# A ranking step of an attention kernel moved from VectorE to GpSimd, and its score matmuls cut in two equal halves

## The chip, the cores and the metric

The kernel runs on one core of a Trainium2 chip. The metric is the device time of one launch in microseconds (us). The engines are TensorE (PE, with its weight loads shown apart as PEld), VectorE (DVE), ScalarE (ACT), GpSimd (POOL) and SyncE (SP). Each works through its own instructions in the order in which the program gives them; semaphores tie the engines together.

## The reference

Attention with a top-32 mask comes first, then two mixture-of-experts (MoE) layers on its output:

```python
# q, k, v: batch 2, heads 8, 576 rows, 64 columns
scores = scale * np.matmul(q, k.transpose(0, 1, 3, 2))
kth = np.partition(scores, -32, axis=-1)[..., -32:-31]
scores = np.where(scores >= kth, scores, -1e9)
attn = np.exp(scores - scores.max(-1, keepdims=True))
attn = attn / (attn.sum(-1, keepdims=True) + 1e-9)
out = np.matmul(attn, v)
# then x = out as (1152, 512); per layer: 8 experts, each token goes to its best expert,
# relu(x @ w1[e]) @ w2[e], times the gate's probability; the first layer has a capacity
```

The change lies in the attention part alone: for each row of scores the 32nd largest value is wanted as a threshold.

## The kernel before

Attention works in blocks of 128 rows of scores by 576 keys. Two heads form a unit; a unit has 9 blocks (4 full row tiles of each head, and one block that holds the 64 last rows of both heads and so needs twice the score matmuls). There are 8 units, 72 blocks, numbered by their place in `seq`, and 36 pairs of blocks, numbered k_.

For each block PE multiplies queries and keys into PSUM (`scores`). The keys are held in two parts, a rounded one and its remainder, so a block has two passes. The result goes to two places: keys 512 to 575 beside the transposes in `pt_`, keys 0 to 511 in a bank of `sc`. ACT copies both to SBUF (`s`). DVE reduces a pair's 576 scores to 160 candidates in a row (`folds`: two maxima, two minima, one more maximum, then four searches for the eight largest). Then DVE ranks them (`chain`): four times it takes the eight largest of the candidates into `top`, and between these it replaces the eight that were found by -1e30 (a match-replace, which the trace shows as a load of the values and the replacement). The eighth value of the fourth step is the threshold. The two chains of a pair are interleaved with the folds of the next pair (`woven`).

From the largest value and the threshold POOL forms `nb` (`limits`) and a shifted copy of the scores (`lowered`); ACT forms a mask (`below`). PE transposes the shifted copy and adds the mask in PSUM (`flip`), ACT takes the exponential (`expo`), PE multiplies by the values (`values`), ACT copies the result out.

The program orders this by hand. In iteration i of the main loop PE issues the scores of block i + 4, then the flip of block i - 3, then the values of block i - 4, and then jobs: turning the next unit's queries and keys (`turn`, six times in a unit; `turn_tails`, whose last transpose is L288; `v_turn`; `v_gates`). DVE issues in two iterations the folds of the next pair and the chains of the present one. POOL's queue holds in each iteration the limits, the shifted copy and jobs: the splits of queries and keys, sums, `normed` (whose output SP sends to memory) and `missed`, which notes in `flv` whether a block's candidates could have lost a value. The last four blocks are written out behind the loop: the last two chains run on DVE alone, their rows are kept as they are and transposed by PE. At the end PE sums `flv`; where a block is flagged, a loop (`repair`) does it again. The MoE layers start when attention has ended.

Of the kernel before, what the change touches and what calls it, by code (L numbers as in the profile page):

```python
# [10 lines left out]
F32 = mybir.dt.float32  # L11
F32R = mybir.dt.float32r
BF = mybir.dt.bfloat16
# [3 lines left out]
OP = mybir.AluOpType  # L17
# [5 lines left out]
TOPK = 32  # L23
NEG = -1.0e30
BIG = 2.0 ** 80
EPS = 1e-9
SIZES = [256, 208, 192, 176, 160, 144, 128, 128]
COLS = [(r, t, min(128, n - t * 128)) for r, n in enumerate(SIZES) for t in range((n + 127) // 128)]
# [19 lines left out]
def attn_moe_moe_kernel(ctx, tc, q, k, v, g1, w11, w12, capacity, g2, w21, w22, out):  # L48
# [113 lines left out]
    def attention():  # L162
# [9 lines left out]
        with tc.tile_pool(name="ald", bufs=2) as ld, tc.tile_pool(name="awk", bufs=2) as wk, \  # L172
# [21 lines left out]
            for i in range(4):  # L194
# [2 lines left out]
                nc.gpsimd.memset(v_[:, :, :, D + E:], 1.0)  # L197
                vx.append(v_)
            flv = wk.tile([128, NU, NT, 2], F32, name="flv", bufs=1)
            xb = ps.tile([128, 512], F32, name="xb")  # L200
            pt_ = ps.tile([128, NC * 128], F32, name="pt")
            rest_read = []
            xo = xb[:, :6 * XW].rearrange("p (g h w) -> p g h w", h=2, w=XW)
            zero = wk.tile([128, RW], F32, name="zero", bufs=1)
# [100 lines left out]
            def scores(u, t):  # L305
                z = st[u]
                if tiles[t] is not None:
                    hh, c = tiles[t]
                    ops = [(z["qk"][:, hh, 0, c * 128:(c + 1) * 128], z["qk"][:, hh, j]) for j in (1, 2)]
                else:  # L310
                    qt = z["qtail"].rearrange("p h s -> p (h s)")
                    ops = [(qt[:, hh * 128:hh * 128 + 128], z["qk"][:, hh, j]) for hh in range(2) for j in (1, 2)]
                k_, j_ = divmod(seq.index((u, t)), 2)
                z_ = pair(k_)
                sc, s = z_.sc, z_.s
                places_ = ((pt_[:, M * 128:S], slice(M * 128, S)), (sc[:, j_], slice(0, M * 128)))
                for n_, (l, r) in enumerate(ops):
                    for w_, (o, w) in enumerate(places_):
                        m_ = nc.tensor.matmul(o, l, r[:, w], start=(n_ == 0), stop=(n_ == len(ops) - 1))  # L319
                        if w_ and j_ and z_.read is not None:  # L320
                            tc.declare_no_dep(m_.ins, z_.read.ins, reason="two banks")
                for w_, (o, w) in enumerate(places_):
                    a_ = nc.scalar.activation(s[:, j_, w], o, AF.Copy)
                    if w_ == 0:
                        rest_read[:] = [a_]
                z_.read = a_
# [28 lines left out]
                            lambda j=j: nc.vector.max(x[:, j, W4 + 8:], z.mn[:, j])]  # L355
                return ops

            def chain(i):
                z = pairs[i // 2]
                x, t8 = z.cand[:, i % 2], z.top[:, i % 2]  # L360
                y = wk.tile([128, CW], F32, name="y")
                ops = []
                for r in range(TOPK // 8):
                    cur = x if r == 0 else y
                    w = t8[:, 8 * r:8 * r + 8]
                    ops.append(lambda w=w, cur=cur: nc.vector.max(w, cur))  # L366
                    if r < TOPK // 8 - 1:
                        ops.append(lambda w=w, cur=cur: nc.vector.match_replace(y, w, cur, NEG))
                return ops

            def woven(chains, fill, order=""):

# [275 lines left out]
            def run_jobs(i, late):  # L648
                for f, a in jobs.get(i, []):
                    if (f in turning or f == wide) == late:  # L650
                        f(*a)
                        flush()
# [2 lines left out]
                run_jobs(i, True)  # L655
            K = L // 2

            def back(k, wait=lambda: None):

                pt = flip(k)  # L660
                wait()
                if k >= 1:
                    value(k - 1)
                pTs[k] = expo(pt)
                if k >= 1:
                    value_out(k - 1)

            def fresh(k):
                lowered(*ranges(k))
                return lambda: below(*ranges(k))  # L670
# [14 lines left out]
            def keep(k, e):  # L685
                z = pairs[k // 2]
                nc.vector.scalar_tensor_tensor(kept[k % 2][:, :S], z.s[:, k % 2], z.top[:, k % 2, TOPK - 1:], e,
                                               op0=OP.is_ge, op1=OP.mult)

            for i in range(L - 4):  # L690
                k_, j_ = divmod(i, 2)
                if j_ == 0 and k_ >= 1:
                    limits(k_ - 1)
                relu = fresh(i - 2) if i >= 2 else lambda: None
                run_jobs(i, False)
                scores(*seq[i + 4])
                if k_ == 0:
                    vec = woven((chain(i), []), folds(j_, (1,) if j_ == 0 else (0, 1)))
                elif j_ == 0:
                    todo = woven((chain(i), chain(i + 1)), folds(k_ + 1, (0, 1)))  # L700
                    vec, todo = todo[:12], todo[12:]
                else:
                    vec = todo
                do(vec)
                if i >= 3:
                    back(i - 3, relu)
                else:
                    relu()
                run_jobs(i, True)
                if i < 4:  # L710
                    wide_spin((6, 6, 6, 3)[i], xb)
                elif i == 4:
                    spin(12, free)
# [20 lines left out]
            value_out(L - 5)  # L734
            pTs[L - 4] = expo(flip(L - 4))
            run_jobs(L - 3, True)
            limits(K - 2, slice(1, 2))
            relu = fresh(L - 3)
            a, b = chain(L - 2), chain(L - 1)
# [1067 lines left out]
```

## Time and profile before

| what | us |
|---|---|
| median of 3 runs (lowest, highest) | 613.36 (613.05, 617.69) |
| the profiled execution, its own time | 613.21 |
| its span, first to last instruction | 611.6 |
| DVE busy | 501.1 (82%) |
| PE busy | 587.1 (96%) |
| ACT busy | 417.5 (68%) |
| POOL busy | 191.9 (31%) |

The span is what the profile shows; about 1.6 us lie around it. The busy shares are means over the whole span, and the attention stage fills only its first 268 us or so. The ends of matmuls are modelled, so PE's work is better read from the distance between the starts of its instructions. "Idle before" is time in which the engine did nothing ahead of an instruction, with the instruction that ended it. The granted clock of TensorE was 0.986 of its full 2.4 GHz as a mean over the span.

### The profile page before, as it was taken

The page shows a single profiled execution, that of the slowest core. Times are in us where ns is not written, and L with a number is a line of the kernel's source. Part 1 is how long each engine was busy: PE and PEld are TensorE (multiplying, and loading weights), DVE is VectorE, ACT ScalarE, POOL GpSimd, SP SyncE. Part 2 cuts the span into 40 slices and gives each one's busy share as a digit, 9 for nine tenths or more (in the row PEclk, how much of TensorE's full clock was granted, in tenths as well). Part 3 has the DMA queues.
Part 4 walks back from the last instruction along what each step waited for, and adds up shares of the span by engine and source line. Part 5 has one row for each costly group of instructions (what it writes and reads, how often), then busy time and mean ns, then how long its engine had stood idle before and what let it go on. Part 6 is the DMA issues. An engine that isn't in the chain of part 4 may idle for free.

```text
span 611.6 us, 13886 instructions
## 1 busy us (share of the span) xinstructions
PE 587.1 (96%) x4789; PEld 545.5 (89%) x4789; DVE 501.1 (82%) x1729; ACT 417.5 (68%) x970; POOL 191.9 (31%) x423
## 2 busy tenths in 40 slices
PE   8999999999999998879899999999999999999995
PEld 5789999999999988767799999999999899999994
DVE  6989999999999999974967778873478788788750
ACT  6668888888888876622776777764265678787650
POOL 8565554745374233424020200100012302111010
PEclk9989999999999999989899999999999999999999
DMA  6630332234350000019795568768276975777660
GB/s 144 158 70 10 109 95 81 70 91 71 103 51 18 4 18 4 10 38 303 268 342 211 187 232 241 238 232 294 107 240 217 343 258 189 264 267 253 220 217 14
DMA packets 78639, 96.04 MB, mean 157 GB/s; under 512 B 33797, under 2 KB 40453, under 8 KB 78560
## 3 DMA queue, kind: packets, MB, share of 16 engines
q1 hardware_dynamic: 73632, 84.07, 44.0%
q0 software_dynamic: 3728, 10.70, 5.4%
q8 instruction: 40, 0.66, 0.4%
q10 hardware_dynamic: 1200, 0.30, 0.2%
q14 instruction: 39, 0.32, 0.2%
HBM read 82.32 MB, written 13.22 MB: 156 GB/s over the span
## 4 chain that ended last, share of the span: by engine, by line
PE 37%; DMA 10%; issue 5%; DVE 1%; POOLq 0%; ACT 0%; POOL 0%; SPq 0%; ACTq 0%; DVEq 0%
PE pp L1095 8%; DMA out_dram<-yr,sidx 8%; PE pp L1134 7%; PE pp L1097 3%; PE pp L1136 3%; PE pp L1088 2%; DMA raw<-in_moe_w_dram 2%; PE pl L1148 1%; PE pt L1052 1%; PE pp L1128 1%; PE pp L1132 1%; PE pp L1130 1%; PE pp L1131 1%; PE pp L1091 1%; PE pp L1093 1%
## 5 line engine op out<-in xcount | busy, mean ns | idle before, releaser
L423 PE MATMUL xb<-vx,pT 128*128 128x73 f32 (+1 forms) x800 | 94.6, 267 | 0.4 <-ACT xl L436 0.4
L1095 PE MATMUL pp<-xT,w1c 128*128 128x416 f32 (+4 forms) x320 | 93.9, 362 | 0.5 <-DVE xT L1058 0.5
L423 PEld LDWEIGHTS xb<-vx,pT 128*128 128x128 f32 (+1 forms) x800 | 87.7, 182 | 2.7 <-issue 1.1
L1134 PE MATMUL pp<-hT,w2c 128*128 128x416 f32 (+4 forms) x320 | 88.0, 353 | 0.0
L1023 DVE TENSOR_TENSOR w2c<-raw,w2c 128x512 fp32r<-128x512 f32 x112 | 74.1, 685 | 16.8 <-ACT w2c L1022 16.6
L1136 PE MATMUL pp<-hT,w2c 128*128 128x208 f32 (+4 forms) x320 | 78.4, 245 | 0.0
L1097 PE MATMUL pp<-xT,w1c 128*128 128x208 f32 (+4 forms) x320 | 77.8, 243 | 0.0
L1023 DVE TENSOR_TENSOR w1c<-raw,w1c 128x512 fp32r<-128x512 f32 x96 | 60.9, 686 | 14.2 <-ACT w1c L1022 13.9
L1022 ACT ACTIVATE w2c<-raw 128x512 fp32r<-128x512 f32 x112 | 66.7, 623 | 6.7 <-PE pp L1136 3.7
L402 PE MATMUL pt<-ident,shifted 128*128 128x128 f32 x350 | 67.8, 279 | 0.6 <-ACT pT L411 0.3
L1074 ACT ACTIVATE t<-pp 128x208 f32<-128x208 f32 (+4 forms) x120 | 37.6, 314 | 41.3 <-PE pp L1097 29.6
L403 PE MATMUL pt<-negid,under 128*128 128x128 bf16 x350 | 63.8, 220 | 0.3 <-ACT under L393 0.3
L1022 ACT ACTIVATE w1c<-raw 128x512 fp32r<-128x512 f32 x96 | 53.5, 621 | 13.2 <-DMA raw<-in_moe_w_dram 7.1
L1095 PEld LDWEIGHTS pp<-xT,w1c 128*128 128x128 f32 x320 | 60.1, 188 | 1.5 <-DVE xT L1058 0.9
L1136 PEld LDWEIGHTS pp<-hT,w2c 128*128 128x128 f32 x320 | 61.2, 191 | 0.0
L1097 PEld LDWEIGHTS pp<-xT,w1c 128*128 128x128 f32 x320 | 61.1, 191 | 0.0
L1134 PEld LDWEIGHTS pp<-hT,w2c 128*128 128x128 f32 x320 | 60.2, 188 | 0.0
L366 DVE MAX8 top<-y 128x8 f32<-128x160 f32 x216 | 59.1, 313 | 0.0
L393 ACT ACTIVATE under<-s,nb 128x576 bf16<-128x576 f32 x70 | 53.7, 768 | 6.4 <-POOL nb L385 6.4
L402 PEld LDWEIGHTS pt<-ident,shifted 128*128 128x128 f32 x350 | 49.3, 141 | 5.2 <-POOL nb L680 0.8
L396 POOL TENSOR_SCALAR shifted<-s,nb 128x576 f32<-128x576 f32 x70 | 52.0, 746 | 4.1 <-POOL nb L385 0.2
L319 PE MATMUL sc<-qkT 128*128 128x512 f32 x128 | 53.0, 480 | 0.0
(332 smaller groups left out, 1447.5 us busy)
## 6 DMA issues: line engine op xcount, KB each, us to landing
raw<-in_moe_w_dram SPq DMA_DIRECT2D x62, 1024.0 KB, 5.5
out_dram<-zero SPq DMA_DIRECT2D x3, 768.0 KB, 3.8
y<-yr POOLq DMA_DIRECT2D x8, 256.5 KB, 4.2
kraw<-in_k_dram SPq DMA_DIRECT2D x8, 256.0 KB, 3.4
vraw<-in_v_dram SPq DMA_DIRECT2D x16, 128.0 KB, 2.9
vx<-in_v_dram SPq DMA_DIRECT2D x16, 128.0 KB, 2.6
w2c<-in_moe_w_dram SPq DMA_DIRECT2D x4, 512.0 KB, 8.0
x<-xn SPq DMA_DIRECT2D x15, 128.0 KB, 1.8
```

The costliest lines, as they stand in the source:

```text
L319: m_ = nc.tensor.matmul(o, l, r[:, w], start=(n_ == 0), stop=(n_ == len(ops) - 1))
L366: ops.append(lambda w=w, cur=cur: nc.vector.max(w, cur))
L393: nc.scalar.activation(under[k % 3][:, :S], s, AF.Relu, bias=nb[:, 1:2], scale=-BIG)
L402: both = (nc.tensor.matmul(pt[:, o], shifted[k % 3][:, o], ident, is_transpose=True, start=True, stop=False), nc.tensor.matmul(pt[:, o], u ...
L403: nc.tensor.matmul(pt[:, o], under[k % 3][:, o], negid, start=False, stop=True))
L423: nc.tensor.matmul(o, pT[:, c2, cols], z["v"][:, c2, hh], start=(c2 == 0), stop=(c2 == NC - 1))
L1022: nc.scalar.activation(o[:, 0], src_, AF.Copy)
L1023: nc.vector.tensor_tensor(o[:, 1], src_, o[:, 0].bitcast(F32), op=OP.subtract)
L1095: nc.tensor.matmul(ph[:, :2 * n].rearrange("p (w n) -> p w n", w=2), w[f][:, 0, d], xT[:, d, :, :n], start=st, stop=False)
L1097: nc.tensor.matmul(ph[:, :n], w[f][:, 1, d], xT[:, d, 0, :n], start=False, stop=sp)
L1134: nc.tensor.matmul(py[:, :2 * n].rearrange("p (w n) -> p w n", w=2), w[f][:, 0, o], hT[:, f, :, :n], start=st, stop=False)
L1136: nc.tensor.matmul(py[:, :n], w[f][:, 1, o], hT[:, f, 0, :n], start=False, stop=sp)
```

## The change

For pairs 2 to 33 the first removal of each chain leaves DVE. The first eight maxima (`heads`) are taken at the end of the DVE work of the pair before. POOL compares the candidates with the eighth value, writes 2^100 where a candidate is at least as large and 0 elsewhere (`gone`, bf16), and subtracts that from the candidates (`removed`). The chains go on from the second maximum (`tails_of`), behind the folds instead of interleaved with them. A tie at the eighth place would remove more than eight, so PE counts the removed in each pair by four matmuls with one column (`counted_out`), between the flip and the values. `ties` adds the counts up and raises the flags of a pair with too many; it stands behind the flip of block 68, ahead of the last two chains.

The score matmuls write keys 288 to 575 and then keys 0 to 287, both passes of a half one after the other. The right half has a place of its own behind the transposes' PSUM tile.

```diff
+OUT = 2.0 ** 100
...
+            unit = wk.tile([128, 1], BF, name="unit", bufs=1)
+            nc.gpsimd.memset(unit, 1.0 / OUT)
+            ones_f = wk.tile([128, 128], F32, name="ones_f", bufs=1)
+            nc.gpsimd.memset(ones_f, 1.0)
...
-            pt_ = ps.tile([128, NC * 128], F32, name="pt")
+            both_ = ps.tile([128, NC * 128 + W2], F32, name="pt")
+            pt_, right_ = both_[:, :NC * 128], both_[:, NC * 128:]
...
-                places_ = ((pt_[:, M * 128:S], slice(M * 128, S)), (sc[:, j_], slice(0, M * 128)))
-                for n_, (l, r) in enumerate(ops):
-                    for w_, (o, w) in enumerate(places_):
+                places_ = ((right_, slice(W2, S)), (sc[:, j_, :W2], slice(0, W2)))
+                for w_, (o, w) in enumerate(places_):
+                    for n_, (l, r) in enumerate(ops):
...
-            def chain(i):
+            def chain(i, first=0, y=None):
...
-                y = wk.tile([128, CW], F32, name="y")
+                y = wk.tile([128, CW], F32, name="y") if y is None else y
-                for r in range(TOPK // 8):
+                for r in range(first, TOPK // 8):
...
+            def heads(k_):
+                z = pairs[k_]
+                return [lambda j=j: nc.vector.max(z.top[:, j, :8], z.cand[:, j]) for j in range(2)]
+
+            def removed(k_):
+                z = pairs[k_]
+                z.gone = wk.tile([128, 2, CW], BF, name="gone")
+                z.y = wk.tile([128, 2, CW], F32, name="ypair")
+                for j in range(2):
+                    nc.gpsimd.tensor_scalar(z.gone[:, j], z.cand[:, j], z.top[:, j, 7:8], OUT, op0=OP.is_ge, op1=OP.mult)
+                nc.gpsimd.tensor_tensor(z.y, z.cand, z.gone, op=OP.subtract)
+
+            def tails_of(k_):
+                z = pairs[k_]
+                a, b = (chain(2 * k_ + j, 1, z.y[:, j]) for j in range(2))
+                return [f for ab in zip(a, b) for f in ab]
+
+            def counted_out(k_):
+                g = pairs[k_].gone.rearrange("p j w -> p (j w)")
+                n = CW // 2
+                for c in range(4):
+                    nc.tensor.matmul(free[:n, k_:k_ + 1], g[:, c * n:c * n + n], unit, start=(c == 0), stop=(c == 3))
+
+            def ties():
+                n = slice(FIRST, PAIRED)
+                c = wk.tile([CW // 2, PAIRED], F32, name="gone_n", bufs=1)
+                nc.scalar.activation(c[:, n], free[:CW // 2, n], AF.Copy)
+                nc.tensor.matmul(rest[:, 1, n], ones_f[:CW // 2], c[:, n], start=True, stop=True)
+                o = flv.rearrange("s u t w -> s (u t) w")[:, 2 * FIRST:2 * PAIRED, 0].rearrange("s (k j) -> s k j", j=2)
+                nc.vector.scalar_tensor_tensor(o, rest[:, 1, n][:, :, None].to_broadcast([128, PAIRED - FIRST, 2]),
+                                               -2 * 128 * 8 - 0.5, o, op0=OP.add, op1=OP.max)
...
-            def back(k, wait=lambda: None):
+            def back(k, wait=lambda: None, then=lambda: None):
                 pt = flip(k)
                 wait()
+                then()
...
+            FIRST, PAIRED = 2, K - 2
             for i in range(L - 4):
                 k_, j_ = divmod(i, 2)
                 if j_ == 0 and k_ >= 1:
                     limits(k_ - 1)
                 relu = fresh(i - 2) if i >= 2 else lambda: None
+                if j_ == 0 and FIRST <= k_ < PAIRED:
+                    removed(k_)
                 run_jobs(i, False)
                 scores(*seq[i + 4])
...
                 elif j_ == 0:
-                    todo = woven((chain(i), chain(i + 1)), folds(k_ + 1, (0, 1)))
+                    if k_ < FIRST:
+                        todo = woven((chain(i), chain(i + 1)), folds(k_ + 1, (0, 1)))
+                    else:
+                        todo = folds(k_ + 1, (0, 1)) + tails_of(k_)
+                    if FIRST <= k_ + 1 < PAIRED:
+                        todo += heads(k_ + 1)
...
-                    back(i - 3, relu)
+                    back(i - 3, relu, (lambda: counted_out(k_)) if j_ and FIRST <= k_ < PAIRED else lambda: None)
...
             pTs[L - 4] = expo(flip(L - 4))
             run_jobs(L - 3, True)
+            ties()
             limits(K - 2, slice(1, 2))
```

## Rows read from the trace of the kernel before

**Rows 1.** Windows: time, busy us (x instructions) of PE PEld DVE ACT POOL, clock, DMA.
```profile
60.00:90.00 30.00, 30.00 (x277) 27.96 (x276) 30.00 (x129) 25.10 (x56) 16.45 (x35) 1.00 0.35 103
...
210.00:240.00 30.00, 28.60 (x250) 25.71 (x249) 30.00 (x129) 22.27 (x50) 11.12 (x26) 1.00 0.04 11
```

**Rows 2.** Timeline of DVE, one pair: start us, duration us, engine, line, operation.
```profile
133.94 0.43 DVE L348 TENSOR_TENSOR hi<-sc,s 128x288 f32<-128x288 f32 x1
...
135.12 0.07 DVE L368 MATCH_VALUE_LOAD y<-top,cand 128x8 f32 x1
...
135.70 0.74 DVE L350 TENSOR_TENSOR lo<-sc,s 128x576 f32<-128x576 f32 x1
...
140.77 0.43 DVE L348 TENSOR_TENSOR hi<-sc,s 128x288 f32<-128x288 f32 x1
```

**Rows 3.** Timeline of PE: scores behind turned tails, and a late wait.
```profile
62.79 0.30 PE L319 MATMUL pt<-qkT 128*128 128x64 f32 x1
...
90.78 1.29 PE L423 MATMUL xb<-vx,pT 128*128 128x73 f32 x10
...
92.72 0.30 PE L319 MATMUL pt<-qkT 128*128 128x64 f32 x1
...
214.50 0.30 PE L319 MATMUL pt<-qkT 128*128 128x64 f32 x1
...
245.16 0.30 PE L319 MATMUL pt<-qkT 128*128 128x64 f32 x1 [1.00 <-ACT pT L411]
```

**Rows 4.** Timeline of PE: a turning, one block's scores, the next flip.
```profile
82.72 0.52 PE L255 MATMUL pg<-identr,qs 128*128 128x128 f32 x4
83.08 0.27 PE L319 MATMUL pt<-qkT 128*128 128x64 f32 x1
...
83.49 0.19 PE L319 MATMUL pt<-qkT 128*128 128x64 f32 x1
...
83.84 0.27 PE L402 MATMUL pt<-ident,shifted 128*128 128x128 f32 x1
```

**Rows 5.** Timeline of PE: runs of short matmuls (weights rows*columns, then moving).
```profile
77.56 1.48 PE L423 MATMUL xb<-vx,pT 128*64 128x73 f32 x20
...
81.64 1.29 PE L423 MATMUL xb<-vx,pT 128*128 128x73 f32 x10
...
274.52 0.77 PE L1318 MATMUL pi<-r,onehot 128*128 128x28 bf16 x10 [1.89 <-DVE r L1299]
```

**Rows 6.** Timeline of PE: first and last of eight matmuls of 256 columns.
```profile
293.42 0.28 PE L1092 MATMUL pp<-xT,w1c 128*128 128x256 f32 x1
...
294.24 0.28 PE L1093 MATMUL pp<-xT,w1c 128*128 128x256 f32 x1
```

**Rows 7.** POOL's groups by form: count | busy us, mean ns | idle before.
```profile
L396 POOL TENSOR_SCALAR shifted<-s,nb 128x576 f32<-128x576 f32 x70 | 52.0, 746 | 4.1 <-POOL nb L385 0.2
L244 POOL TENSOR_TENSOR ks<-kraw,ks 128x512 fp32r<-128x512 f32 x7 | 9.0, 1282 | 0.6
...
L385 POOL TENSOR_TENSOR nb<-top,coef 128x4 f32<-128x4 f32 x34 | 6.8, 199 | 102.7 <-DVE top L366 73.3 <-ACT s L323 13.5 <-PE pt L403 11.7
...
L247 POOL TENSOR_SCALAR ks<-kraw 64x128 fp32r<-64x128 f32 x14 | 4.1, 291 | 0.0
...
L244 POOL TENSOR_TENSOR ks<-kraw,ks 64x128 fp32r<-64x128 f32 x7 | 3.2, 453 | 0.6
```

**Rows 8.** Timelines of DVE, PE and ACT at the end of attention.
```profile
257.36 0.53 DVE L366 MAX8 top<-cand 128x8 f32<-128x160 f32 x2
...
262.06 0.82 DVE L687 SCALAR_TENSOR_TENSOR kept<-s,top,e 128x576 f32<-128x576 f32 x1
...
257.34 0.33 PE L402 MATMUL pt<-ident,shifted 128*128 128x128 f32 x1
...
263.56 0.71 PE L773 MATMUL sc<-ident,kept 128*128 128x128 f32 x5
...
258.51 0.70 ACT L411 ACTIVATE pT<-pt 128x640 f32<-128x640 f32 x1 [0.77 <-PE pt L403]
```

## The prediction

> **What bounds the kernel now.** The windows view, cut by stretch, shows the attention stage with VectorE (DVE) busy for 30.00 of 30 us from 60 to 240 us, and TensorE (PE) busy for 30.00 early and 28.60 late [rows 1]. A busy share of PE does not show whether it is at its limit, so the second look is the order in time of both engines, where the reader is to read distances between starts. On DVE two blocks (a pair) take 6.83 us, from the fold that begins one pair to the fold that begins the next [rows 2]; that is 4.5 x 6.83 = 30.74 us for a unit of 9 blocks. On PE the scores behind the turned tails come at 62.79 and 92.72: 29.93 us for a unit [rows 3]. So PE has only 0.8 us in 30 to spare. The stage has two bounds nearly on top of each other, and that decides this change: what is taken off DVE counts only as far as PE follows.
>
> How far PE waits at all: five units from 62.79 to 214.50 took 151.71 us, and at 29.93 each they need 149.65, so 2.1 us of waiting [rows 3]. From 214.50 to 245.16 it took 30.66 us. This last unit has no six turnings (0.36 us each, 82.72 to 83.08 [rows 4]) and no turned tails (values from 90.78 to scores at 92.72 is 1.94, of which the values are 1.08 by 81.64 to 82.72, so 0.86 [rows 3 to 5]); its work is 29.93 - 2.16 - 0.86 = 26.9, and it waits 3.8 us, the 1.00 us in the last of rows 3 among them. Together 5.9 us: with a DVE that costs nothing, PE alone would save about that.
>
> **The change part by part.** The sum goes against the profiled execution: 613.21 us, span 611.6; the median of the runs is 613.36, 0.15 above.
>
> DVE: for 32 pairs (2 to 33) two match-replaces go. From the first load of values at 135.12 to the next fold at 135.70 they hold DVE 0.58 us [rows 2], 18.6 us in all. The pair falls to 6.25 us, the unit to 28.1. The first max of each chain is moved, not added: it runs at the end of the pair before, and gives GpSimd (POOL) the time of the folds to work in. The folds begin a pair now in one piece; the other 12 steps of a pair are chain steps of at most 0.29 us (half of the 0.58), 3.5 in all, so the folds take at least 2.8 us. This whole gain is covered by PE; it is worth only PE's waits, 5.9 us.
>
> PE, scores: a block has two passes, one for each part of the keys, and a pass now streams 288 and 288 columns instead of 64 and 512. Behind the start stand 68 blocks, eight of them with double work: 76 blocks' worth. One pass of the old form takes 83.49 to 83.84 = 0.35 us [rows 4]: the 64 columns cost nearly a whole weight load. At 256 columns matmuls follow each other by (294.24 - 293.42)/7 = 0.117 us [rows 6]; scaled to 288 that is 0.132. A pass becomes 0.264, a block saves 2 x 0.086 = 0.17, and 76 x 0.17 = 13.1 us. Bounds: the whole old block, 83.08 to 83.84, is 0.76 against 4 x 0.132, so 0.23 and 17.5 us; from below I let each matmul keep 0.165, for a start that the weights don't reach in time, 0.04 a block and 3 us.
>
> PE, counting: four matmuls for each of 32 pairs, one column moving, 80 weight columns in bf16. With so little moving, the spacing is the weight load. Nearest rows: ten bf16 matmuls of 28 columns in 0.77 us, 0.07 each with its tail; fp32 weights of 64 columns 1.48/20 = 0.07, of 128 columns 1.08/10 = 0.11 [rows 5]. I take 0.07 and 0.02 for the value weights that no longer load behind a flip: 0.30 a pair, 9.6 us. Bounds 0.03 each (half of the bf16 row for fewer columns), 0.13 a pair, 4 us; and 0.11 each, 0.45, 14.4 us. They are issued between the flips and the values of the odd block. They wait for POOL's comparison, which belongs to a pair whose maxima ended about one PE block pair earlier; that wait is covered by some 5 us. If it were not, the values, their copy on ScalarE and the next flip would queue behind it. The Trainium skill, TensorE: Matmul & The Clock Gate, section Weight-path perf modes, gives the fast weight load only to 128 columns that are not fp32, and its LDWEIGHTS section has columns/1.2 ns otherwise: by it 80 columns are 0.067 us and the sum is the same 9 us, and the cheap rival below falls; no row here has 80 bf16 columns.
>
> ScalarE copies 288 + 288 instead of 64 + 512 columns, the same sum. The right copy can start earlier, since its two matmuls are first; DVE's first fold needs only that one. Nothing is counted.
>
> POOL: two comparisons of 160 and a subtraction of 320 columns per pair. Tensor-scalar took 0.291 for 128 and 0.746 for 576, so 0.35 for 160; tensor-tensor 0.453 for 128 and 1.282 for 512, so 0.87 for 320 [rows 7]: 1.57 a pair. POOL was busy 16.45 us in 30 [rows 1] and goes to 16.45 + 4.5 x 1.57 = 23.5 in 29.3. They stand ahead of the splits, the next shifted copy and the DMA issues of POOL's jobs; those move by 1.6 us and their users come a block later. After the last maximum of a pair POOL has nb (0.2), a shifted copy (0.75) and these [rows 7], 2.5 us, against at least 2.8 of folds on DVE. So no stall, with a margin of 0.3 us at least; past it the tails of both chains would stand behind the subtraction on DVE, and PE's flips two blocks later. Two small memsets at the start are hidden behind loads.
>
> The end: one new wait. The check of ties puts a copy on ScalarE behind the exponential of block 68, a small matmul behind that, and a DVE step ahead of the last two chains. Flip 68 starts at 257.34, its exponential runs 258.51 to 259.21, while DVE began the last chains at 257.36 [rows 8]. With about 0.9 us for copy, matmul and step (an estimate from like short steps), DVE begins them at 260.1, 2.7 later. Of this 0.7 is free: the last kept row is ready at 262.06 + 0.82 = 262.88 and PE comes to it at 263.56 [rows 8]. Price 2.0 us, in full whenever DVE arrives first. Queued behind it: both last chains, then transposes, values, the whole second stage. The two MoE stages start from the end of attention and just move.
>
> Sum: - 5.9 (PE's waits) - 13.1 (scores) + 9.6 (counts) + 2.0 (ties) = -7.4; 613.2 - 7.4 = **606 us**. DVE stays below PE: 28.1 against 29.93 - 10 x 0.17 + 4.5 x 0.30 = 29.6 for a unit.
>
> **Rivals.** (a) Counting is dear or the halves save little: at 14.4 us for counts the sum is -2.6, 610.6; with 6 us saved in the scores as well it is +4. I take 610 to 614 for this. For it: a load of 128 fp32 columns takes 0.11 [rows 5]. Against: the bf16 row there. (b) Counting is cheap, 4 us: 613.2 - 13 = 600. (c) Slower: POOL becomes the bound. Place: the comparison and subtraction ahead of the tails of each chain. If the three steps take 3.5 us a pair instead of 1.57, POOL needs 16.45 + 15.8 = 32.2 us a unit, 1.5 over the old 30.74; over 7.1 units that is +10.5, and with the tie wait 626. It decides against the change from (30.74 - 16.45)/4.5 = 3.2 us a pair on. For it: no comparison with a scalar from SBUF and a bf16 result stands in the trace. Against: the same engine's multiply-add forms are twice inside the limit. The Trainium skill, GPSIMD Engine Reference, section Engine selection, speaks against the move: two-input elementwise work is about twice as slow there as on VectorE. The trace doesn't contradict it, and twice slow is still under the limit. (d) DVE's whole 18.6 arrives, 597: against it stands PE's 29.93.
>
> **How the numbers follow.** A measurement tells 1% from no change, so faster is below 607.2, slower above 619.5. Forecast (602 to 610): 0.50, of which 0.38 below 607.2. (a) 0.21. (b) and (d) 0.14. (c) 0.12; the rest, 0.03, is mishaps above 614 but within 1%. Faster 0.52, same 0.35, slower 0.13. The range 600 to 614 leaves out (c), part of (b) and (d), and the rest.
>
> **What would show it.** Right: PE starts of scores behind turned tails about 29.6 apart, DVE with idle time ahead of the first fold, ended by ScalarE's copy of the right half; score matmuls of 288 about 0.13 apart; counting about 0.3 a pair; DVE idle about 2 us or more at the tie step. Wrong: DVE waits for POOL's subtraction, POOL busy throughout, or PE waits ahead of the counts; or a count spacing far from 0.07.

## The result: 0.7% slower, and the profile after

The changed kernel took **619.02 us** (median of 13 runs, 618.08 to 619.95), the kernel before 614.52 beside it (13 runs, 611.78 to 619.30): a ratio of 1.0067 (of the means), 95% interval 1.0043 to 1.0091. The profiled execution took 619.56 us, its span 617.9 against 611.6. The forecast was 606, its range 600 to 614.

The windows of the changed kernel, in the columns of [rows 1], show what changed places:

```profile
60.00:90.00 30.00, 28.43 (x287) 27.31 (x286) 27.06 (x105) 23.57 (x54) 25.97 (x44) 1.00 0.35 104
...
210.00:240.00 30.00, 28.72 (x280) 27.15 (x279) 29.66 (x117) 22.51 (x52) 21.35 (x39) 1.00 0.04 12
```

DVE, which had no idle time, now has 3 us of it in 30, and PE 1.6: both have less to do, and the time didn't fall. POOL went from 16.45 to 26. The waits between 60 and 210 us (engine, tile and line that waited <- what ended the wait: us in total, times, longest) say whom they wait for:

```profile
DVE top L372 <- POOL ypair L389: 10.2, 9, 1.6
ACT under L435 <- POOL nb L427: 9.7, 13, 1.4
...
PEld pt L444 <- POOL shifted L438: 4.6, 6, 1.2
```

L389 is the subtraction, L427 the limits, L438 the shifted copy: all three of POOL's products in this stage are waited for. The first row is one of the prediction's own signs of being wrong. The groups of POOL between 60 and 240 us, beside [rows 7]:

```profile
L388 POOL TENSOR_SCALAR gone<-cand,top 128x160 bf16<-128x160 f32 x53 | 43.8, 827 | 4.8
L438 POOL TENSOR_SCALAR shifted<-s,nb 128x576 f32<-128x576 f32 x52 | 38.9, 748 | 2.8
L389 POOL TENSOR_TENSOR ypair<-cand,gone 128x320 f32<-128x320 f32 x26 | 20.7, 796 | 2.2
```

A comparison of 160 columns takes 0.83 us, more than a shifted copy of 576. The removal costs 2 x 0.83 + 0.80 = **2.45 us** a pair, not 1.57. Two pairs on DVE's timeline (columns as [rows 2]; of the first only the wait is shown), the first behind a split of the next unit's keys, the second quiet:

```profile
126.12 0.55 DVE L372 MAX8 top<-ypair 128x8 f32<-128x160 f32 x2 [1.61 <-POOL ypair L389]
...
199.21 0.43 DVE L354 TENSOR_TENSOR hi<-sc,s 128x288 f32<-128x288 f32 x1
199.68 0.47 DVE L355 TENSOR_TENSOR sc<-sc,s 128x288 f32<-128x288 f32 x1
200.18 0.76 DVE L356 TENSOR_TENSOR lo<-sc,s 128x576 f32<-128x576 f32 x1
...
205.72 0.43 DVE L354 TENSOR_TENSOR hi<-sc,s 128x288 f32<-128x288 f32 x1
```

The quiet pair takes 205.72 - 199.21 = 6.51 us and waits for nothing. By the starts of such folds, pairs near splits take 7.3 to 8.4, in each unit that has splits. From 50 to 193 us 20 pairs take 7.13 on average, 6.86 in the kernel before (from 52 to 189): there the change loses what it gains elsewhere. What POOL does around the wait at 126.12:

```profile
121.91 0.29 POOL L253 TENSOR_SCALAR ks<-kraw 64x128 fp32r<-64x128 f32 x1
...
122.33 0.20 POOL L427 TENSOR_TENSOR nb<-top,coef 128x4 f32<-128x4 f32 x1
122.63 0.75 POOL L438 TENSOR_SCALAR shifted<-s,nb 128x576 f32<-128x576 f32 x1
123.47 1.74 POOL L388 TENSOR_SCALAR gone<-cand,top 128x160 bf16<-128x160 f32 x2
125.30 0.79 POOL L389 TENSOR_TENSOR ypair<-cand,gone 128x320 f32<-128x320 f32 x1
126.07 0.74 POOL L438 TENSOR_SCALAR shifted<-s,nb 128x576 f32<-128x576 f32 x1
```

It works without a wait; a split's last piece ends at 122.2, and from the limits at 122.33 to the end of the subtraction at 126.09 are 3.8 us. DVE's folds, from 199.21 to the next tails at 202.73, take 3.5. In a quiet pair POOL begins its limits ahead of the folds and the removal is just in time; behind a split it begins late, and the removal is too. On PE, scores and counts (the last two rows of another block):

```profile
127.11 0.51 PE L325 MATMUL pt<-qkT 128*128 128x288 f32 x2
127.46 0.42 PE L325 MATMUL sc<-qkT 128*128 128x288 f32 x2
127.72 0.27 PE L444 MATMUL pt<-ident,shifted 128*128 128x128 f32 x1
...
125.46 0.28 PE L401 MATMUL xb<-unit,gone 128*80 128x1 bf16 x4
125.60 0.42 PE L465 MATMUL xb<-vx,pT 128*128 128x73 f32 x2
```

A block's scores take 127.72 - 127.11 = 0.61 us instead of 0.76 [rows 4] (0.62 is common among the blocks), four counts 125.60 - 125.46 = 0.14. The end of attention (beside [rows 8]), PE and then DVE:

```profile
258.49 0.33 PE L444 MATMUL pt<-ident,shifted 128*128 128x128 f32 x1
...
260.50 0.41 PE L408 MATMUL sc<-gone_n,ones_f 80*128 80x32 f32 x2 [0.93 <-ACT gone_n L407]
261.30 0.81 PE L536 MATMUL sc<-idle,ones 128*128 128x512 bf16 x3 [0.39 <-DVE flv L410]
261.94 0.27 PE L444 MATMUL pt<-ident,shifted 128*128 128x128 f32 x1
...
266.75 0.77 PE L825 MATMUL sc<-ident,kept 128*128 128x128 f32 x5 [0.39 <-DVE kept L730]
...
271.78 0.63 PE L1260 MATMUL pp<-idle,ones 128*128 128x64 bf16 x16 [1.58 <-ACTq L872]
```
```profile
261.02 0.22 DVE L410 SCALAR_TENSOR_TENSOR flv<-sc,flv 128x64 f32<-128x64 f32 x1 [2.67 <-PE sc L408]
```

The expert stages of the kernel before begin with this row of PE, of the same kind as the row at 271.78:

```profile
268.62 0.63 PE L1208 MATMUL pp<-idle,ones 128*128 128x64 bf16 x16 [1.58 <-ACTq L820]
```

The difference in span, 6.3 us, has three parts. The flip of block 68 starts at 258.49 instead of 257.34 [rows 8]: the main loop ends 1.2 us late (2.6 against a second profile of the kernel before, see experiment 1), where the forecast had it 9.4 early (5.9 + 13.1 - 9.6). DVE then stands idle 2.67 us for the tie check, and the turning of the last kept row comes at 266.75 instead of 263.56: 3.2 us with the 1.2. The other 3.1 lie in the two expert stages, which the change doesn't touch; from the row at 268.62 or 271.78 to the end they took 343.0 before and 346.1 in the change, and from 343 to 347.1 us in all profiles together. The granted clock was lower there in the change (0.77 of full against 0.83 from 270 to 300 us, 0.97 against 1.00 from 360 to 420), but the halves alone (experiment 1) took 346.5 with 0.83 and 1.00. What sets this stays open, so what follows goes by ratios to the kernel before, run beside each, and where that is too coarse by the start of the expert stages.

### The profile page after: what moved, and what is told of

It is laid out like the page before. It is cut to its first block, busy times and chain, and to the rows that moved or that the text cites. A ratio compares the mean times of both kernels' runs of the same rounds, so it can differ in the third digit from the quotient of the medians.

```text
span 617.9 us, 14118 instructions
## 1 busy us (share of the span) xinstructions
PE 585.8 (95%) x4919; PEld 550.0 (89%) x4919; DVE 490.5 (79%) x1602; ACT 411.3 (67%) x971; POOL 270.0 (44%) x521
## 4 chain that ended last, share of the span: by engine, by line
PE 38%; DMA 8%; issue 5%; DVE 3%; ACT 1%; POOL 0%; POOLq 0%; DVEq 0%; ACTq 0%
DMA out_dram<-yr,sidx 8%; PE pp L1147 7%; PE pp L1186 7%; PE pp L1149 3%; PE pp L1188 3%; PE pp L1140 2%; PE pt L1104 2%; PE pl L1200 1%; PE pp L1144 1%; PE pp L1143 1%; PE pp L1145 1%; PE pp L1180 1%; PE pp L1260 1%; PE pp L1184 1%; PE pp L1182 1%
## 5 line engine op out<-in xcount | busy, mean ns | idle before, releaser
L1147 PE MATMUL pp<-xT,w1c 128*128 128x416 f32 (+4 forms) x320 | 95.5, 366 | 0.5 <-DVE xT L1110 0.5
L1075 DVE TENSOR_TENSOR w1c<-raw,w1c 128x512 fp32r<-128x512 f32 x96 | 60.7, 684 | 10.6 <-ACT w1c L1074 10.3
L1147 PEld LDWEIGHTS pp<-xT,w1c 128*128 128x128 f32 x320 | 60.9, 190 | 1.9 <-DVE xT L1110 0.9
L372 DVE MAX8 top<-ypair 128x8 f32<-128x160 f32 x192 | 52.2, 313 | 12.5 <-POOL ypair L389 12.3
L1149 PEld LDWEIGHTS pp<-xT,w1c 128*128 128x128 f32 x320 | 61.8, 193 | 0.0
L1567 POOL DMA_DIRECT2D y<-yr x13 | 7.3, 564 | 121.0 <-issue 56.5
L1249 POOL DMA_INDIRECT out_dram<-yr,sidx x14 | 13.6, 972 | 103.9 <-ACT yr L1230 90.1
```

The costliest lines, as they stand in the source:

```text
L1075: nc.vector.tensor_tensor(o[:, 1], src_, o[:, 0].bitcast(F32), op=OP.subtract)
L1147: nc.tensor.matmul(ph[:, :2 * n].rearrange("p (w n) -> p w n", w=2), w[f][:, 0, d], xT[:, d, :, :n], start=st, stop=False)
L1149: nc.tensor.matmul(ph[:, :n], w[f][:, 1, d], xT[:, d, 0, :n], start=False, stop=sp)
```

## The experiments

**Theory A:** the comparison is dear, so POOL's products come late. Rivals: the halves, the tie check at the end, or the counts lose it.

**1. The parts alone.** Before plus the halves:

```diff
-places_ = ((pt_[:, M * 128:S], slice(M * 128, S)), (sc[:, j_], slice(0, M * 128)))
+places_ = ((right_, slice(W2, S)), (sc[:, j_, :W2], slice(0, W2)))
```


> The kernel before with the scores as two halves and nothing else. Theory A (VectorE's 30.74 us a unit and GpSimd's queue set the pace, PE's savings are covered): the pair stays at 6.83 us, only stretches where PE is late (the start) gain, 1 to 3 us: 611 to 613 where the kernel before has 614.5, ratio about 0.996. By the prediction's terms alone (PE 29.93 - 1.5 a unit) DVE's 30.74 would bound it, so at most PE's 5.9 us of waits turn into gain elsewhere: not under 608. Rival B (the halves themselves harm, since the right half shares its bank with the turned block and the copy order changes): slower than before, 616 or more.


Measured: 613.67 us, ratio **0.9985** (0.9969 to 1.0002). They do no harm and gain next to nothing in the whole; DVE (third pair of figures) has 30.00 of 30 us, and the pair stayed at 6.79 to 6.95, as before:

```profile
60.00:90.00 30.00, 29.15 (x280) 27.94 (x279) 30.00 (x130) 24.11 (x54) 15.77 (x33) 1.00 0.35 104
```

In the profile the expert stages begin at 265.79, 2.8 us early. Nearly all of it was won by 52 us: the kernel before had there two pairs of 8.93 and 7.22 us, with 2.3 us of waiting by DVE for ScalarE's copies and a granted clock of 0.74 from 40 to 44 us; here these pairs take 6.83 and the clock is 1.00. The probe of experiment 2 holds a second profile of the kernel before, with the clock at 1.00 there: pairs of 7.34 and 7.22, 0.7 us of waiting, and expert stages from 267.18. So about half of the 2.8 us goes with that fall of the clock in the one profile, and the other 1.4 may be the halves'.

The change with the old form of the scores, otherwise whole:

> The change without the halves: removal on GpSimd, counts and tie check stay. Theory A (GpSimd's 2.5 us a pair is the loss): pairs with splits still take 7.3 to 8.3 us, DVE waits for the subtraction and PE for shifted copies as in the change; PE has its slow scores as well, so 619 to 624, ratio to before 1.008 to 1.015. Rival B (the halves are what harms): at or below the kernel before, 608 to 614. Rival C (only the tie wait at the end loses): 617, ratio 1.004.


Measured: 619.45, ratio **1.0097** (1.0075 to 1.0119). The loss is there without the halves: it belongs to the removal with its counts and its check.

The change without the tie check:
```diff
-            ties()
```


> The change without the check of ties at the end (copy on ScalarE, small matmul and VectorE step left out, so ties go unnoticed); the counts on TensorE stay. Theory A: VectorE begins the last two chains about 2.7 us earlier, some 2.5 to 3 us come back and no more: 616 to 617, still not below the kernel before. Rival C (the tie wait is the whole loss, the removal itself gains 7 to 9 us as predicted): 606 to 610. Rival D (it was covered: kept rows were early enough): 618.5 to 619.


Measured: 616.88, ratio **1.0038** (1.0014 to 1.0063), 0.29% or 1.8 us below the change's ratio. The two intervals overlap, but in the profiles the expert stages begin 2.5 us earlier (269.31 for 271.78). So the price of 2.0 was about right, and is not the whole loss.

**2. The price by itself.** Forms of POOL's work appended to the kernel before:
```diff
+forms = [lambda: pts(gb[:, 0], a, w, P, op0=OP.is_ge, op1=OP.mult),
...
+         lambda: pts(gf[:, 0], a, w, P, op0=OP.add, op1=OP.mult),
...
```


> The kernel before, with forms of GpSimd's work appended behind its end, four of each, while all other engines rest: comparison and multiplication of 160 columns to bf16 and to fp32, addition and multiplication to bf16 and fp32, the comparison at 16, 80 and 320 columns, and subtractions of 320 columns with fp32, bf16 and repeated operands. Theory A1 (the comparison is dear by itself): 0.83 us to bf16 and to fp32, 0.35 for the additions, and 320 columns about twice of 160. Rival A2 (the bf16 result is dear): 0.83 for both operations to bf16, 0.35 to fp32. Rival A3 (it is contention with VectorE in the stage): 0.35 for all here. The subtraction: 0.79 in all three forms. The run as a whole is some 30 to 40 us longer than the kernel before, which means nothing.


Measured, with the other engines at rest (start, duration of the group, line, form; of the group ahead of these, the change's own form, two of four records are missing):

```profile
611.00 3.57 POOL L1791 TENSOR_SCALAR gf<-x,t 128x160 f32<-128x160 f32 x4
614.65 1.89 POOL L1792 TENSOR_SCALAR gb<-x,t 128x160 bf16<-128x160 f32 x4
616.61 1.89 POOL L1793 TENSOR_SCALAR gf<-x,t 128x160 f32<-128x160 f32 x4
618.57 1.67 POOL L1794 TENSOR_SCALAR gb<-x,t 128x16 bf16<-128x16 f32 x4
...
622.93 5.71 POOL L1796 TENSOR_SCALAR gb<-x,t 128x320 bf16<-128x320 f32 x4
628.72 2.42 POOL L1797 TENSOR_SCALAR gf<-x,t 128x320 f32<-128x320 f32 x4
```

L1791, L1794 and L1796 compare, L1792, L1793 and L1797 add. From start to start a comparison takes 0.44 us at 16 columns (the group behind it begins at 620.34), 0.91 at 160 and 1.45 at 320 (5.79/4), an addition 0.49 at 160 and 0.62 at 320 (the next group begins at 631.22). A column costs (1.45 - 0.44)/304 = 3.3 ns in a comparison and (0.62 - 0.49)/160 = 0.8 ns in an addition. So it is the operation: not the bf16 result (the comparison to fp32 is as dear, the addition to bf16 cheap), nor contention with DVE. Theory A1 had two figures wrong: an addition costs 0.49, not 0.35, and the comparison of 320 takes 1.6 times that of 160, not twice. The subtraction of two tensors of 320 takes 0.94 with an fp32 and 0.87 with a bf16 operand.

**3. The change at the predicted price.** Comparisons cut to 16 of the 160 columns, so that this kernel leaves most of the removal out and ranks other values:
```diff
-nc.gpsimd.tensor_scalar(z.gone[:, j], z.cand[:, j], z.top[:, j, 7:8], OUT, op0=OP.is_ge, op1=OP.mult)
+nc.gpsimd.tensor_scalar(z.gone[:, j, :16], z.cand[:, j, :16], z.top[:, j, 7:8], OUT, op0=OP.is_ge, op1=OP.mult)
```


> The change with its comparisons cut to the first 16 of 160 columns (so most large candidates stay in and the ranking is not the reference's); order, waits, counts and tie check stay. By the appended forms such a comparison takes about 0.41 us instead of 0.83, and the removal 0.41 + 0.41 + 0.79 = 1.61 us a pair: the price that the prediction took (1.57). Theory A (the price of the comparison is the loss): VectorE's waits for the subtraction fall from 22.5 us between 45 and 250 to under 6, GpSimd to 22 of 30, quiet pairs from 6.51 to 6.25-6.35, pairs behind splits under 7; 611 to 614 in all, of it 3 us the tie wait. Rival F (where the removal stands in GpSimd's queue, behind and ahead of the splits, whatever its price): split pairs stay at 7.3 to 8.3, 616 to 618.


Measured: **605.85** us, ratio 0.9864 (0.9825 to 0.9902), a larger gain than the 611 to 614 of theory A. POOL's group, two folds, and the first row of the expert stages:

```profile
L391 POOL TENSOR_SCALAR gone<-cand,top 128x16 bf16<-128x16 f32 x54 | 18.8, 348 | 4.9
```
```profile
126.90 0.44 DVE L357 TENSOR_TENSOR hi<-sc,s 128x288 f32<-128x288 f32 x1
...
133.41 0.43 DVE L357 TENSOR_TENSOR hi<-sc,s 128x288 f32<-128x288 f32 x1
```
```profile
257.91 1.01 PE L1263 MATMUL pp<-idle,ones 128*128 128x64 bf16 x16 [1.58 <-ACTq L875]
```

The removal takes 2 x 0.35 + 0.80 = 1.49 us. The pairs from 29 to 231 us take 6.46 to 6.63, those near splits too (theory A had 6.25 to 6.35 for quiet ones), and DVE's waits for the subtraction are gone from the list. The expert stages begin 13.9 us ahead of the change's. Rival F, that its place in the queue loses whatever the price, falls; and since the counts are all there, so does the rival that they lose it.

**4. The tie step's place.**
```diff
             keep(L - 1, es[1])
+            tied()
```


> The change whole, only VectorE's step of the tie check moved from ahead of the last two chains to behind the last kept row; ScalarE's copy and the small matmul stay where they are. Theory A: the same 2.1 to 3 us as leaving the check out, 616 to 617: the wait was the place of the step and not its work. Rival G (copy and matmul cost, not the step's place): 618.5 to 619.


Measured: 622.45, ratio **1.0126** (1.0085 to 1.0166), a miss on the other side. The timeline of PE says why:

```profile
263.56 1.44 PE L539 MATMUL sc<-idle,ones 128*128 128x512 bf16 x3 [3.09 <-DVE flv L413]
264.79 0.42 PE L447 MATMUL pt<-ident,shifted 128*128 128x128 f32 x1
```

Three filler matmuls write the other bank of the tile that the step reads, and are ordered behind it; block 69's turning stands behind them. In the change this is the 0.39 us at 261.30; moved late, it is 3.09. The last kept row comes 5.0 us later than in the change, more than the wait adds. From 259.1 to 263.56 PE had only the small matmuls at 260.06 to do; the granted clock is 0.62 of full from 262 to 264 us and 0.50 (1.2 GHz) from 264 to 272, and the five transposes of that row take 1.19 us, not 0.77:

```profile
271.74 1.19 PE L829 MATMUL sc<-ident,kept 128*128 128x128 f32 x5
```

The fillers freed (`declare_no_dep`, two banks):

> As the run with VectorE's tie step late, but the three filler matmuls behind it, which write another bank of the same PSUM tile, no longer are ordered behind that step. Theory A: the turning of block 69 no longer stands behind fillers that wait for VectorE (264.8 there, 261.9 in the change, 260.1 without the check), it starts near 260, and the time is that of the run without the check: 616 to 617.5. Rival G (copy and small matmul themselves delay PE): 619 or more.


Measured: 616.80, ratio **1.0022** (0.9996 to 1.0047): as without the check, whose interval it overlaps. So in the change the place of one step costs 2 to 3 us, late and with the fillers behind it some 6 (1.0126 against 1.0022), and its work nothing that shows.

**5. POOL relieved by ScalarE.**
```diff
+nc.scalar.activation(r, z.cand[:, 1], AF.Relu, bias=z.top[:, 1, 7:8], scale=-1.0)
+nc.scalar.activation(z.gone[:, 1], r, AF.Exp, bias=lnout, scale=-BIG)
```


> The change with the tie step late, and the comparison of every second chain taken from GpSimd to ScalarE (a Relu of the limit minus the candidates, and an exponential that makes 2^100 of zero and nothing of the rest, 160 columns each); GpSimd keeps one comparison and the subtraction: 0.83 + 0.79 = 1.62 us a pair, about what the prediction assumed. ScalarE gets two steps of about 0.3 us a pair, 2.7 us a unit, 23.5 to 26.5 of 30. Theory A: waits for the subtraction fall under 8 us, quiet pairs to 6.3, 607 to 611. Rival H (ScalarE waits for the first maxima and all its copies and exponentials queue behind): PE waits for copies and exponentials, 615 or more.


Measured: 627.15, ratio **1.0221** (1.0174 to 1.0267); it has the late tie step of experiment 4 with its loss, 1.0126. Rival H holds: it is slower even than that, and from 60 to 210 us the waits are

```profile
POOL ypair L393 <- ACT gone L392: 22.0, 18, 1.9
PEld pt L451 <- ACT s L331: 13.1, 21, 0.8
DVE top L374 <- POOL ypair L393: 8.8, 15, 0.7
```

**6. More time for the removal.** The first maxima right behind the folds, the removal half a pair earlier:
```diff
-todo = folds(k_ + 1, (0, 1)) + tails_of(k_)
+todo = folds(k_ + 1, (0, 1)) + (heads(k_ + 1) if k_ + 1 < PAIRED else []) + tails_of(k_)
```


> The change with the same instructions, GpSimd's dear comparisons among them, in another order: the first maximum of each chain of a pair stands on VectorE directly behind that pair's folds, ahead of the tails of the pair before, and GpSimd gets the removal in the odd block, half a pair earlier. The removal then has some 6 us instead of about 3.2 until the tails read it. Theory A (the removal's 2.45 us are too long for the window it was given): pairs of 6.51 everywhere as with the cheap comparisons, no waits of VectorE for the subtraction, 606 to 609. Rival I (GpSimd's load itself, 26 of 30 us, delays the shifted copies, and PE with them): pairs behind splits stay over 7 us, PE waits for shifted copies, 612 to 617.


Measured: 616.74, ratio **1.0029** (1.0000 to 1.0057). No wait for the subtraction is left, but theory A's 606 to 609 fell and rival I's 612 to 617 held. From 60 to 210 us the pairs take 6.5 to 6.8, but for three of 8.0 to 9.1. The waits moved:

```profile
DVE rs L484 <- POOL rs L504: 8.4, 4, 3.4
ACT under L435 <- POOL nb L427: 7.9, 6, 2.3
```

With the late tie step and free fillers as well:

> Both repairs: first maxima directly behind the folds, and the tie step late with free fillers. Theory A: the time of the run with the first alone less 2 to 3 us: 603 to 606, ratio to before about 0.985. Rival I: 610 to 615.


Measured: 615.06, ratio **0.9995** (0.9966 to 1.0024): rival I's range again. And with that wait for the unit's sums taken out too (the step a block later):

> Both repairs (first maxima directly behind the folds, tie step late and free), and the step behind a unit's sums moved a block later (but for the last two units), so that VectorE's reciprocal no longer stands right behind GpSimd's total, which queues behind the removal. In the run without this VectorE waited four times, 8.4 us, for that total between 60 and 210. Theory L (that single wait): the pairs of 9.1 and 10.2 us go to under 7, 615.06 - 7 to 9: 606 to 608.5. Rival I (the load of GpSimd as such): the wait comes back elsewhere, 611 to 615.


Measured: 614.53, ratio **0.9984** (0.9953 to 1.0015). Theory L fell: that wait is gone from the list, but ScalarE's for the limits is nearly what it was (10.8 in the run without the step moved), and DVE now waits for ScalarE's copies of the scores, which the list of that run doesn't have:

```profile
ACT under L438 <- POOL nb L430: 9.4, 6, 2.3
...
DVE hi L354 <- ACT s L329: 7.6, 7, 1.7
```

From 60 to 210 us POOL, in order, is 24 to 28 us busy in 30 in these three runs; with one product on time another is late. Window alone is not enough.

**7. Weaving.** The last maxima of a pair between the first folds of the next:
```diff
+do([f_[0], held[0], f_[1], held[1]])
```


> Both repairs, and the last maximum of each of the two chains of a pair woven between the first folds of the next (fold, maximum, fold, maximum). In all forms of the change a quiet pair takes 6.51 us where 6.83 - 0.58 = 6.25 was predicted: the first two folds stand back to back and take 0.47 and 0.50 from start to start, where they took 0.31 and 0.36 behind a maximum. Theory J (that is VectorE's whole 0.26): pairs of 6.25 to 6.3, 8 us over 31 pairs less what PE holds back, 598 to 603. Rival K (PE is at its end at 6.5 a pair: 30.00 us busy in 30 with the cheap comparisons): pairs stay at 6.45 to 6.55, 603 to 606.


Measured: 613.71, ratio **0.9955** (0.9924 to 0.9987). Both theories' times fell, but theory J is right on DVE, in a quiet pair:

```profile
218.66 0.45 DVE L354 TENSOR_TENSOR hi<-sc,s 128x288 f32<-128x288 f32 x1
219.02 0.32 DVE L372 MAX8 top<-ypair 128x8 f32<-128x160 f32 x1
...
224.96 0.46 DVE L354 TENSOR_TENSOR hi<-sc,s 128x288 f32<-128x288 f32 x1
```

6.30 us from fold to fold (6.24 to 6.37 from 206 us on, where POOL has no splits), near the predicted 6.25; ahead of that they take 6.0 to 8.7. The same with the unit's sums a block later took 614.87, ratio 0.9986 (0.9959 to 1.0014), no better.

**8. Without POOL's limits.** On the last kernel of experiment 7, the shifted copy subtracts, instead of adding a negated limit:
```diff
-nc.gpsimd.tensor_scalar(shifted[k % 3][:, :S], s, nb[:, 0:1], 1.0, op0=OP.add, op1=OP.mult)
+nc.gpsimd.tensor_scalar(shifted[k % 3][:, :S], s, nb[:, 0:1], 1.0, op0=OP.subtract, op1=OP.mult)
```


> The same, and GpSimd's limits step (two products of 2 columns a pair, 0.2 us each) is gone: the shifted copy subtracts the largest score directly, ScalarE's clipped copy takes the 32nd score as it is, and the factor 2^80 sits in the matrix it is turned with. ScalarE's clipped copies then wait for VectorE alone. Theory M (ScalarE's wait for GpSimd's limits is what delays the score copies): the 7.0 and 8.5 us of waits fall under 3 each, 603 to 607. Rival I (the shifted copies still queue behind removal and splits, so PE waits for them instead): 609 to 613.


Measured: 681.94, ratio **1.1099** (1.1055 to 1.1143). Neither theory had this row:

```profile
L438 POOL TENSOR_SCALAR shifted<-s,top 128x576 f32<-128x576 f32 x39 | 86.3, 2215 | 0.2
```

The same copy takes 2.22 us with a subtraction and 0.75 with an addition: per column the price of the comparison again, if about 0.3 us is taken off each ((2.22 - 0.3)/576 = 3.3 ns). POOL was 28.5 to 28.8 of 30 us busy throughout.

**9. POOL relieved where it is full.** The removal in 22 pairs, the ten near splits as before the change:
```diff
+AWAY_K = [k_ for k_ in range(FIRST, PAIRED) if k_ not in (5, 6, 9, 10, 14, 15, 18, 19, 23, 24)]
```


> The change with the tie step late, and the removal on GpSimd only in 22 of 32 pairs; the ten pairs next to which GpSimd prepares the next unit's keys and queries (5, 6, 9, 10, 14, 15, 18, 19, 23, 24) rank as before, wholly on VectorE. In the change these ten take 74.3 us by the starts of the folds, 12 over the quiet ones. Theory A: they fall to about 6.83 each, 68.3, the quiet ones stay at 6.5; 616.9 - 6 to 9: 608 to 611, and VectorE's waits for the subtraction to under 8 us. Rival F2 (the quiet pairs now collide with what moved up, or PE's waits take the place): 613 to 617.


Measured: 614.46, ratio **1.0017** (0.9989 to 1.0045), rival F2's range, with the late tie step and the fillers that wait for it: the last folds began at 242.7, block 69 was turned only at 256.6. With free fillers:

> The removal on GpSimd in 22 of 32 pairs, as in the earlier run of that kind, with the tie step late and the three fillers no longer ordered behind it. In that earlier run the last folds began at 242.7 (before: 250.4), and then block 69 was turned only at 256.6, 6.8 us behind block 68. Theory A with I (GpSimd's load where splits fall is the loss, the tie step's place the rest): block 69 near 252.7, second-to-last kept row turned at 256 to 256.5 where before it was 262 to 263.6: 607 to 610, ratio 0.988 to 0.993. Rival (the gain is lost in the stages behind, as with the halves alone): 612 to 614.


Measured: **606.57** us where the kernel before had 611.43, ratio **0.9934** (0.9910 to 0.9959): 0.7% below the kernel before, and the whole interval is below 1. Rows of its PE and of POOL's windows (fifth pair of figures):

```profile
252.64 0.27 PE L447 MATMUL pt<-ident,shifted 128*128 128x128 f32 x1
...
256.27 0.71 PE L833 MATMUL sc<-ident,kept 128*128 128x128 f32 x5
```
```profile
60.00:90.00 30.00, 29.58 (x292) 28.50 (x291) 29.86 (x125) 24.66 (x56) 20.57 (x38) 1.00 0.36 106
```

The last kept row is turned at 256.27, 7.3 us before [rows 8]; DVE has 29.86, and its wait for the subtraction is gone from the list of 60 to 210 us. POOL is 20.6 us busy here, but 25.3 in the next 30 us, near the change's 26.4 there: where its work stands matters as well as how much it is. Ten other pairs as a control were not tried; in the change's trace quiet pairs wait for nothing. Two variants stayed within 0.1% of it: the removal half a pair earlier, 607.16 (0.9932), and ScalarE's clipped copy without POOL's limit, 607.03 (0.9938), for which 1 to 3 us less had been expected.

## Why the prediction was wrong, step by step

**The step that failed** is POOL's: "So no stall, with a margin of 0.3 us at least". The comparison was priced at 0.35 from multiply-add forms of other widths; it took 0.83, and the removal 2.45 us instead of 1.57. That is past the margin of 0.3, and the folds' 3.5 us, 0.7 over the bound of 2.8, save only the quiet pairs: behind a split DVE waits for the subtraction, 10.2 us in 9 waits. The sum had this term at nothing. Experiment 3 shows what it is: at 1.49 a pair, all other steps kept, the ratio is 0.9864 and not 1.0067, some 12.5 us.

**Luck in the 606.** Experiment 3 also lands on the forecast, in part by luck. By the measured prices below, scores and counts give 6.1 us and not 3.5, so the sum would have been -10.0. In its profile the expert stages do begin 9.3 to 10.7 us early (257.91 against 267.18 and 268.62 in the two profiles of the kernel before), but then took 345.4 us where they took 343.0: a forecast short by 2.6 us met stages longer by 2.4.

**The threshold of rival (c) failed too.** The mechanism and its place were the right ones, but it was to decide only from 3.2 us a pair on. That divided POOL's work evenly over a unit. At 2.45 POOL is still idle 4 us in 30; the loss comes where splits stand in its queue, and there limits, shifted copies and subtraction are late together. The outcome, slower but within 1%, fell into what the prediction left to mishaps, with a chance of 0.03. Experiment 6 gave the removal more window and moved the waits; experiment 9 took it from those pairs and got the gain. The rival's time, 626, was for 3.5 us a pair and is not to be set against 619. That it is the load in those pairs is shown by experiments 3 and 9; which of the three late products costs how much stays open. A wait of ScalarE for the limits need cost nothing: the halves alone have 15.4 us of it from 60 to 210, more than the change, with pairs as before.

**The two bounds** were read rightly, as far as this was tried: the halves alone save PE 0.14 a block and leave DVE's pair as it was (experiment 1), and with the removal at a low price the two give 8 us (experiment 3). That fits the prediction's point that each counts only as far as the other engine follows; the removal at a low price without the halves was not run.

**DVE's pair** fell to 6.51, not 6.25. Two match-replaces went, but the first folds now stand back to back and take 0.47 and 0.50 from start to start (199.21, 199.68, 200.18 above), where each took 0.35 to 0.36 before, with a maximum behind it. (The expectation in experiment 7 says 0.31 for the first; that is so in a few pairs only.) Experiment 7 got 6.24 to 6.37. That loss was covered in the forecast, since 4.5 x 6.51 = 29.3 is below the 29.6 that PE was given. By the measured prices PE needs 29.93 - 10 x 0.14 + 4.5 x 0.14 = 29.2, so the two end level.

**PE's scores:** 0.13 between matmuls (127.46 to 127.72 for two) was predicted as 0.132; the first of a block takes 0.22 (127.11 to 127.46 for two, less 0.13), so a block saves 0.14 instead of 0.17, 10.6 us for 13.1. **Counts:** 0.14 a pair against 0.30, 4.5 us instead of 9.6, near the lower bound. Together PE got 6.1 us where 3.5 were forecast. Of the counts, the trace speaks against the rule that the prediction cited from the Trainium skill, TensorE: Matmul & The Clock Gate, section LDWEIGHTS, by which 80 columns are 0.067 us: the spacing is 0.03 to 0.04.

**The tie wait** was 2.67 us of DVE's idle time and cost 1.8 by the ratios and 2.5 by the profiles, near the predicted 2.0 (experiment 1). Missed was that PE's fillers wait for the step as well (experiment 4).

The Trainium skill, GPSIMD Engine Reference, section Engine selection, calls one-input work on that engine roughly line-rate. The addition here agrees (0.75 us for 576 columns, where a fold of 576 on VectorE takes 0.76 above); the comparison and the subtraction with a scalar, also one-input, do not (3.3 ns).

## What to carry to other kernels

Price an operation on an engine by a row of that very operation: the engine and the form of the instruction were the same here, the arithmetic was not, and it made a factor of four per column. An engine that works in order can be late long before it is busy all the time, here at 26 us of 30; look at the stretch where its queue is longest, and put new work in the others. A small check at a joint costs by where its step stands and by what the ordering of a shared tile ties to it, not by its work; a wait that lets PE stand idle can cost more than its length (experiment 4).

## What the runs showed of the hardware

On GpSimd a one-input step with a scalar from SBUF costs about 0.3 us and then 0.8 ns a column for addition and multiplication (0.746 us for 576), but 3.3 ns for a comparison (0.827 for 160) and for a subtraction (2.215 for 576). The comparison's price is the same with DVE at rest and busy (0.91 from start to start in experiment 2; two of them in 1.74 us in the change). On TensorE, four bf16 weight loads of 80 columns with one moving column each follow each other in 0.14 us.
